# Long-convolution block with adaptive norm: the first norm, the filter's first block and the first convolution interleaved on two-sided pools

## The chip, the core and the metric

The kernel runs on one core of one Trainium2 chip. A core has TensorE (PE, matrix products, with its weight load shown apart as PEld), VectorE (DVE), ScalarE (ACT), GpSimd (POOL) and SyncE (SP, which here only starts transfers). Each engine takes its own instructions in order and waits on semaphores for the others. The metric is device time in microseconds of one execution; the median of three runs counts. Times of places in the trace are microseconds from the first instruction.

## What is computed

One input of 2048 positions by 576 channels runs through a convolution block and a feed-forward block. Each has a norm in front, scaled and shifted by vectors made from a condition, and a gated sum behind. Cut to what matters:

```python
mod = (_silu(c) @ w_mod).reshape(c.shape[0], 6, 1, -1)
sa, ca, ga, sb, cb, gb = (mod[:, i] for i in range(6))
h = _layernorm(x) * (1 + ca) + sa
# per channel: dt = exp(log_dt), A = -exp(log_A_real) + i A_imag, C = (C_real + i C_imag) dt
K = 2.0 * einsum("dn,dnl->dl", C, exp(A * dt * pos)).real      # 128 states, 2048 positions
y = irfft(rfft(h, 4096) * rfft(K, 4096))[:2048] + h * D_skip
x = x + ga * y
h = _layernorm(x) * (1 + cb) + sb
x = x + gb * (relu(h @ w1) @ w2)                               # 576 to 4608 to 576
```

## The kernel before

The 2048 positions are cut into four blocks of 512, each held as 128 partitions by four. The convolution is done by blocks: block s takes the spectra of filter blocks 0 to s and of input blocks s to 0. The 576 channels are in two halves of 288, called p.

**Filter, first block** (`KGen.first`). The filter's 512 first values per channel come from two tables of powers of exp(A dt): W2 (32 powers) and W1 (16 powers, scaled by C). The channels are cut into six groups g of 96, taken two by two (`CHUNKS`). For a pair, `raw` makes on ACT the phases' integer parts and on DVE their fractions (`turns`, L116), then the exponentials on ACT (`exps`). `values` of a group takes sines and cosines on ACT, multiplies them by the exponentials on DVE (L151, L152, the sines' half, read from PSUM) and on POOL (the cosines' half, recorded at L59) and stores W2 and a small table zs through SP's queue. In its odd half, `start` (L167) makes W1's first entry; POOL computes a product called tc for it at L178 and DVE adds at L158. `make` doubles W1 four times (`doubling`, L224 to L228, the last step's sums on POOL), stores W1, and lets PE form 384 products of 32 by 16 (`products`, L236). `rows` copies them out of PSUM, and after three groups `store` writes half a filter block to memory (kd). Everything that goes through `KGen.act` and `KGen.pool` keeps its order on its engine; the rest of every engine's stream is ordered by the framework's planner from the program's order and its own estimate of readiness.

**Modulation** (`Body.mod`). Three weight slices are loaded at the start; sigmoid, the broadcast `cb` and the products for ga, ca and sa (L517) stand in the program after the first `raw`. ca and sa already hold the factor ga. The other three vectors are made later (`mod_late`, L519), each with a load on POOL's queue into a single buffer wm.

**First convolution** (`conv(0)`, from `main`). It begins when `first` has ended and the pools of KGen are closed; new pools lie where those lay, and each new tile waits for the old tiles under it. Its order: x2 is loaded on SP; `norm1` takes statistics, square roots (ACT, kept in order) and two DVE passes for h (L728, L729); `transform` of K for half 0, then of U (that is h) for both halves, each of eight products with copies on ACT (L642, L643); `butterfly` in two halves on DVE (L656 to L670); `product` of the spectra (L812 to L818, six ops of 1152 columns); `inverse` (L839 on PE, a DVE addition into x2 at L844); the same for half 1, whose K uses `transform1` (a transform with half of the butterfly done by PE, L681 and L683). Then comes the second norm (L876 to L920), with transposes on PE, which gives the feed-forward part its input xh, xl and xs. The filter's half 1 is loaded by `load_kt` once kd has been written. Spectra are saved on POOL's queue for later blocks: Ud, Rd and, for K, a second copy in Kd.

**Feed-forward part** (`ffn`). For each of 4 times 36 slices of the hidden width, 14 products for the hidden values (L982) and 14 for the output (L1007). Between them `step` lets a share of the other work through: the filter's other blocks (`KGen.rest`) and the convolutions of blocks 1 to 3.

The lines that tie the first convolution to the filter are these:

```python
            with ExitStack() as c2:
                kg.open(c2)
                setup = kg.setup(I)
                last = kg.first(setup, self.mod(kg))
            self.main(ctx, kg, last)
```

Of the kernel before, what the change touches and what calls it, by code (L numbers as in the profile page):

```python
# [18 lines left out]
P = 128  # L19
# [27 lines left out]
class KGen:  # L47
# [13 lines left out]
    def open(self, ctx):  # L61

        pool = lambda n, **kw: ctx.enter_context(self.tc.tile_pool(name=n, bufs=1, **kw))
        self.pa, self.pc, self.pt, self.pw = (pool(f"kg_{x}") for x in "actw")
        self.ps, self.ph = pool("kg_ps", space=PSUM), pool("kg_ph", space=PSUM)
        self.Zp = self.ps.tile([P, 2, 8 * G], F32, name="Zp")
# [31 lines left out]
    def exps(self, w, m):  # L98

        n = len(EXPS[m])  # L100
        e = self.pt.tile([P, 8, 2 * G], F32, tag="E", bufs=6, name=f"E_{w.start}")[:, :n]
        for i, slot in enumerate(EXPS[m]):
            self.act(e[:, i], self.a[:, w], AF.Exp, scale=float(slot))
        return e

    def turns(self, w):

        F = []
        for slots in TURNS:
            n = len(slots)  # L110
            k = self.pa.tile([P, 8, 2 * G], I32, tag="k", bufs=3, name=f"k_{w.start}")
            k = k[:, :n]
# [9 lines left out]
    def abs(self, f):  # L122
        c = self.pt.tile([P, 8, G], F32, tag="c", bufs=3, name="c")[:, : f.shape[1]]
        self.act(c, f, AF.Abs)
        return c
# [4 lines left out]
    def half_values(self, g, W2, E, f, odd):  # L130
# [8 lines left out]
        for u in range(2):  # L139
            s = self.ps.tile([P, 512], F32, tag="s", bufs=2, name=f"s_{2 * g + u}")  # L140
# [26 lines left out]
    def start(self, g, s15, c15):  # L167

        v, p = self.nc.vector.tensor_tensor, self.pool
# [4 lines left out]
        t = self.pc.tile([P, 2, 2, H], F32, tag="Tc", name="tc")  # L174
# [3 lines left out]
        p(t, cc, c15.unsqueeze(1).broadcast_to(cb), op=ALU.mult)  # L178
        for u in range(2):
# [3 lines left out]
        return (  # L183
            (W1[:, :, 0, 0], t[:, 0], T[:, 1], ALU.add),
# [59 lines left out]
    def first(self, setup, mod):  # L244

        nc, k = self.nc, self.k
        self.W1, self.Z, W2s, EF, ke = {}, {}, {}, {}, {}

        def raw(c):
            w = slice(CHUNKS[c][0] * G, CHUNKS[c][1] * G)  # L250
            F, E = self.turns(w), [None] * 5
            for m in (2, 3, 0, 1, 4):
                E[m] = self.exps(w, m)
                if m in (3, 1):
                    yield
            for g in range(*CHUNKS[c]):
                gs = slice((g - CHUNKS[c][0]) * G, (g - CHUNKS[c][0]) * G + G)
                EF[g] = [e[:, :, gs] for e in E], [f[:, :, gs] for f in F]

        def values(g, then):  # L260
# [8 lines left out]
            for u in range(2):  # L269
                nc.sync.dma_start(  # L270
                    out=strips(k.W2d[2 * g + u], 4),
                    in_=W2[u].rearrange("p r (y b) c -> p (r y) (b c)", y=2),
# [6 lines left out]
        def make(g):  # L279
            self.doubling(g)  # L280
            for u in range(2):
                nc.sync.dma_start(
                    out=strips(k.W1d[2 * g + u], 2),
                    in_=self.W1[g][:, u].rearrange("p (y a) r c -> p y (a r c)", y=2),
                )
            ps = self.bank(f"kps_{g}")[:, :384].rearrange("p (q a) -> p q a", a=16)
            for u in range(2):
                self.products(ps, self.W1[g], W2s[g][u], u)

            def rows():  # L290
                if g % 3 == 0:
                    ke[0] = self.pc.tile([P, 16, 72], F32, tag="ke", bufs=1, name=f"ke_{g}")
                qs = slice(24 * (g % 3), 24 * (g % 3) + 24)
                self.act(ke[0][:, :, qs], ps.rearrange("p q a -> p a q"), AF.Copy)
                if g % 3 == 2:
                    self.store(0, g // 3, ke[0].rearrange("p a q -> p (a q)"), nc.sync)

            return rows

        next(mod)  # L300
        for _ in raw(0):
            pass
        next(mod)
        setup()
        rows = [lambda: next(mod), lambda: next(mod)]
        for c, (a, b) in enumerate(CHUNKS):
            for g in range(a, b):
                values(g, rows.pop(0) if g > a else lambda: None)
            rows.pop(0)()
# [880 lines left out]
```

## Time and profile before

| what | value |
|---|---|
| runs | 1440.12, 1443.22 and 1445.3 us; median 1443.22 us |
| profiled execution | 1442.42 us; its span 1440.7 us, mean granted PE clock 0.925 |
| busy over the span | PE 1239.4, PEld 982.6, DVE 880.7, ACT 498.3, POOL 189.3 us |
| 0 to 28 us | DVE busy 11.4, ACT 19.6, POOL 2.7 us |
| 28 to 45 us | DVE busy 12.7, ACT 15.7, POOL 14.6 us |
| 110 to 145 us | PE busy 13.2, DVE 29.3, ACT 13.0, POOL 26.8 us |
| 1416 to 1441 us | PE busy 15.7, DVE 4.4 us |
| transfers | 346.49 MB, mean 241 GB/s |

How to read it: a row of the profile has the line of the kernel, the engine, the operation, "out<-in" by the program's tile names, the tiles' sizes and the count, then the busy time and the mean length of one, and after the bar the engine's idle time ahead of these instructions with what ended most of it. A row in order of time begins with its start and its length in microseconds; in brackets stands the idle time ahead of it. A row by stretches begins with the stretch, then its length, each engine's busy time with the number of instructions, the granted PE clock, the mean share of the DMA engines and GB/s. A row of transfers ends with the microseconds from issue to landing.

### The profile page before, as it was taken

Reading aid. Unit: us, or ns where it says so; the run is one execution under the profiler, and the core shown is the slowest. Engines: PE = TensorE matmul, PEld = TensorE weight load, DVE = VectorE, ACT = ScalarE, POOL = GpSimd, SP = SyncE. Lnnn points to the kernel's source line nnn. Section 1 sums busy time; section 2 is a strip of 40 time slices with the busy share of each in tenths; the row PEclk is TensorE's granted clock in tenths of the full one; section 3 lists DMA queues with packets and bytes.
Section 4 is the critical chain, followed back from the end, with each engine's and each line's share of the span. In section 5 each row is a group of like instructions: output and inputs, shape, how many; then the busy total and the mean of one; then the engine's idle time right before and its main releaser. Section 6 shows DMA issues by size and latency. Waiting matters only on the chain. (4 is left out here: it accounts for less than half of the span.)

```text
span 1440.7 us, 25957 instructions
## 1 busy us (share of the span) xinstructions
PE 1239.4 (86%) x10600; PEld 982.6 (68%) x10600; DVE 880.7 (61%) x1355; ACT 498.3 (35%) x1002; POOL 189.3 (13%) x273
## 2 busy tenths in 40 slices
PE   2423376999989997788999999989999999999997
PEld 1323354777867775566787778767887878888885
DVE  4988488899756688837936779353889431101101
ACT  7784041322221340252234322634322253223221
POOL 2467211010111111011110110010100000000000
PEclk9655587899999999899999999999999999999998
DMA  4666869387698695659877998575989656666661
GB/s 152 230 232 232 271 223 329 99 288 244 209 368 314 212 325 175 241 166 394 287 256 258 336 322 290 162 237 151 370 307 334 203 154 205 205 199 195 197 190 59
DMA packets 135110, 346.49 MB, mean 241 GB/s; under 512 B 23440, under 2 KB 23728, under 8 KB 134992
## 3 DMA queue, kind: packets, MB, share of 16 engines
q1 hardware_dynamic: 107008, 218.82, 46.7%
q0 software_dynamic: 27696, 125.43, 24.0%
q8 instruction: 83, 1.36, 0.4%
q10 hardware_dynamic: 288, 0.59, 0.1%
q14 instruction: 35, 0.29, 0.1%
HBM read 261.04 MB, written 83.76 MB: 239 GB/s over the span
## 5 line engine op out<-in xcount | busy, mean ns | idle before, releaser
L1007 PE MATMUL acc<-hh,w 128*128 128x512 f32 x1296 | 422.4, 400 | 3.0 <-DVE w L968 2.9
L982 PE MATMUL hps<-xh,w 128*128 128x512 f32 x1152 | 398.5, 406 | 0.0
L988 DVE SCALAR_TENSOR_TENSOR hl<-hps,hh 128x512 fp32r<-128x512 f32 x144 | 99.0, 687 | 319.5 <-ACT hh L987 319.2
L1007 PEld LDWEIGHTS acc<-hh,w 128*128 128x128 f32 x1296 | 243.8, 190 | 56.3 <-DVE w L968 3.3
L1007 PE MATMUL acc<-hl,w 128*128 128x512 f32 x720 | 281.3, 401 | 0.1
L982 PEld LDWEIGHTS hps<-xh,w 128*128 128x128 f32 x1152 | 219.7, 192 | 47.3 <-ACT xh L914 0.3
L982 PE MATMUL hps<-xl,w 128*128 128x512 f32 x576 | 232.9, 404 | 0.0
L987 ACT ACTIVATE hh<-hps 128x512 fp32r<-128x512 f32 x144 | 86.0, 598 | 330.4 <-PE hps L982 327.8
L965 ACT ACTIVATE w<-r 128x576 fp32r<-128x576 f32 x144 | 98.9, 687 | 276.9 <-PE acc L1007 216.5
L1007 PEld LDWEIGHTS acc<-hl,w 128*128 128x128 f32 x720 | 136.3, 190 | 29.6 <-DVE hl L988 0.5
L982 PEld LDWEIGHTS hps<-xl,w 128*128 128x128 f32 x576 | 110.2, 191 | 24.1 <-DVE xl L919 0.4
L982 PE MATMUL hps<-xs,w 128*128 128x512 f32 x288 | 104.4, 427 | 19.8 <-ACT w L956 6.6
L956 ACT ACTIVATE w<-r 128x640 fp32r<-128x640 f32 x144 | 105.5, 733 | 36.1 <-DMA L1d<-w 29.4
L236 PE MATMUL kps<-W,W 128*32 128x16 f32 x2304 | 39.8, 219 | 89.6 <-POOL W L59 55.1
L236 PEld LDWEIGHTS kps<-W,W 128*32 128x32 f32 x2304 | 37.6, 151 | 92.1 <-POOL W L59 56.0
L380 PEld LDWEIGHTS kps<-W1r,W2r 128*32 128x32 f32 x3456 | 67.6, 146 | 35.8 <-issue 21.8
L380 PE MATMUL kps<-W1r,W2r 128*32 128x48 f32 (+2 forms) x3456 | 76.5, 238 | 13.0 <-issue 7.4
L818 DVE TENSOR_TENSOR Y<-Y,T 128x1152 f32<-128x1152 f32 x64 | 84.6, 1349 | 0.1
L982 PEld LDWEIGHTS hps<-xs,w 128*128 128x128 f32 x288 | 54.7, 193 | 36.7 <-DVE w L958 7.5
L643 ACT ACTIVATE Z<-ps_f 128x288 f32<-128x288 f32 x120 | 48.3, 413 | 69.0 <-PE ps_f L642 68.3
L1108 POOL DMA_DIRECT2D out_dram<-x x16 | 8.8, 548 | 475.6 <-DVE x L1106 475.6
L642 PE MATMUL ps_f<-kt,fcK 128*128 128x288 f32 x112 | 39.8, 449 | 13.6 <-DVE kt L756 9.6
(200 smaller groups left out, 1422.5 us busy)
## 6 DMA issues: line engine op xcount, KB each, us to landing
r<-in_w_dram SPq DMA_DIRECT2D x144, 320.0 KB, 4.0
r<-in_w_dram SPq DMA_DIRECT2D x144, 288.0 KB, 3.8
w<-L1d SPq DMA_DIRECT2D x108, 320.0 KB, 3.1
w<-L2d SPq DMA_DIRECT2D x108, 288.0 KB, 3.4
W2r<-W2d POOLq DMA_DIRECT2D x18, 1536.0 KB, 10.0
W2d<-W SPq DMA_DIRECT2D x12, 1536.0 KB, 7.5
Ua<-Ud POOLq DMA_DIRECT2D x15, 1152.0 KB, 11.6
W<-W1d POOLq DMA_DIRECT2D x18, 768.0 KB, 9.2
```

The lines of the kernel that those rows point to most:

```text
L236: self.nc.tensor.matmul(ps[32 * dd : 32 * dd + 32, 12 * u + q, :], W2[:, r, :, ch], W1[:, u, :, r, ch], start=(r == 0), stop=(r == 1),)
L380: nc.tensor.matmul(ps[32 * dd : 32 * dd + 32, q, :], W2[:, r, :, ch], W1[:, :, r, ch], start=(r == 0), stop=(r == 1),)
L642: nc.tensor.matmul(o, fc[:, n2, c, :], src(n2), start=True, stop=True)
L643: ev = nc.scalar.activation(Z[:, n2, c], ps[:, :PC], AF.Copy)
L818: v(y, y, T, op=op or ALU.add)
L956: nc.scalar.activation(w[:, 0], r, AF.Copy)
L965: nc.scalar.activation(w[:, 0:D], r, AF.Copy)
L982: nc.tensor.matmul(ps, a, x, start=(i == 0), stop=(i == 13))
L987: nc.scalar.activation(hh, ps, AF.Relu)
L988: nc.vector.scalar_tensor_tensor(hl, ps, 0.0, hh, op0=ALU.max, op1=ALU.subtract)
L1007: nc.tensor.matmul(acc[i], a, x, start=(f == 0 and j in (0, 3, 6, 9, 12)), stop=(f == NF - 1 and j in (2, 5, 8, 11, 13)),)
L1108: nc.gpsimd.dma_start(out=ov[:, n2], in_=x2[:, n2])
```

## The change

- **Pools.** KGen's pools are split. What only the values need (phases, exponentials, the cosines' buffers, the sines' PSUM banks) lies on the left side and is closed early (`early`); W2, W1, the doublings' tiles and the products' PSUM lie on the right side and are closed `late`, inside the first convolution. The feed-forward part's pools then take the right side.
- **First norm.** x is loaded on SP right behind mod's weights. mod runs in front of the first values. The statistics stand ahead of the first values; square roots and the centering (now four ACT ops) stand in the second `raw`; the factor ca and the summand sa become eight POOL ops of 576 columns: two tiles in the second `raw`, one after each of the next two doublings.
- **tc** moves from POOL to DVE.
- **Order.** The transforms of U and K of half 0 stand ahead of the doublings and products of group 4, group 5's doubling stands behind them; then the butterflies of U and K; then group 5's products.
- **Stores.** W2 of group 5 and W1 of groups 4 and 5 are held back until x2 has been asked for, which happens after U's transform of half 1 (x2 and h share a tile).
- **First convolution.** Written out as `conv0` with four fixed spectrum tiles and two PSUM pools (two banks, then four). Kd of block 0 is Rd of block 0, so its second copy is gone. The later blocks' code loses its cases for s = 0.

The core of the diff:

```diff
-    def open(self, ctx):
+    def open(self, early, late):
...
+        self.pa, self.ss = pool(early, "kg_a", "left"), pool(early, "kg_s", "left", space=PSUM)
+        self.pw, self.pc, self.pt = (pool(late, f"kg_{x}", "right") for x in "wct")
+        self.ps, self.ph = (pool(late, f"kg_{x}", "right", space=PSUM) for x in ("ps", "ph"))
...
-        p(t, cc, c15.unsqueeze(1).broadcast_to(cb), op=ALU.mult)
...
+            (t, cc, c15.unsqueeze(1).broadcast_to(cb), ALU.mult),
...
         def raw(c):
             w = slice(CHUNKS[c][0] * G, CHUNKS[c][1] * G)
+            if c == 1:
+                scale()
+            F = self.turns(w)
+            if c == 1:
+                for i in range(4):
+                    center(i)
+                for i in range(2):
+                    affine(i)
+            E = dict((m, self.exps(w, m)) for m in (2, 3, 0, 1, 4))
...
+        def save(dst, src, held):
+            if held:
+                k.held.append((dst, src))
+            else:
+                nc.sync.dma_start(out=dst, in_=src)
...
+        load, stats, scale, center, affine = norm
         next(mod)
+        load()
+        raw(0)
+        for _ in mod:
             pass
         setup()
+        stats()
+        values(0, lambda: None)
+        values(1, lambda: None)
+        for g in (0, 2):
+            raw(g // 2 + 1)
+            for i in (g, g + 1):
+                double(i)
+                if g == 0:
+                    affine(i + 2)
+                multiply(i)
+            values(g + 2, lambda: None)
+            values(g + 3, lambda: rows(g))
+            rows(g + 1)
+        yield
+        double(4)
+        multiply(4)
+        double(5)
+        yield
+        multiply(5)
+        rows(4)
+        rows(5)
...
+        def center(i):
+            kg.act(h[:, i], h[:, i], AF.Identity, scale=rs[i][:, 3:4], bias=rs[i][:, 4:5])
+
+        def affine(i):
+            kg.pool(h[:, i], h[:, i], self.m["ca"], op=ALU.mult)
+            kg.pool(h[:, i], h[:, i], self.m["sa"], op=ALU.add)
...
+    def conv0(self, ctx, c, first, late):
...
+        kt = [self.load_kt(0, 0)]
+        for t, a in zip((fcKn, gcn), I["neg"]):
+            nc.sync.dma_start(out=t, in_=a)
...
+        run(self.transform(lambda n2: hv[:, n2, :, 0], self.fcU, ZU))
+        run(self.transform(src_K(0), self.fcK, ZK))
+        next(first)
+        W = S(2, "W")
+        run(self.butterfly1(ZU, W))
+        U0 = S(0, "U0")
+        run(self.butterfly2(W, U0, -1))
+        self.save(self.Ud[0][0], U0)
...
+        K0 = S(1, "K0")
+        run(self.butterfly2(W, K0, -1))
+        self.save(self.Rd[0][0], K0)
+        next(first, None)
+        kt.append(self.load_kt(0, 1))
+        Z1 = S(2, "Z1")
+        run(self.transform(lambda n2: hv[:, n2, :, 1], self.fcU, Z1))
+        x2 = self.x2[0] = self.x2p[0].tile([P, 4, D], F32, tag="x2", bufs=1, name="x2_0")
+        kept(nc.sync.dma_start(out=x2, in_=I["x"][0].rearrange("n m d -> m n d")))
+        for dst, src in self.held:
+            kept(nc.sync.dma_start(out=dst, in_=src))
+        late.close()
+        self.ff = self.pool(ctx, "ff", side="right")
+        self.xp = [self.pool(ctx, "xa", side="right")]
+        self.cv = cvb = self.pool(c, "cvb")
+        self.cps, self.nps = self.pool(c, "cpsb", space=PSUM, side="right"), 4
...
+        run(self.product(Y, K0, U0, True))
+        V = S(3, "V0")
+        run(self.butterfly1(Y, V))
+        W, U1 = X("W"), None
+        run(self.butterfly1(Z1, W))
+        U1 = S(2, "U1")
+        run(self.butterfly2(W, U1, -1))
+        self.save(self.Ud[0][1], U1)
+        mod = self.mod_late()
+        next(mod)
...
+        run(self.inverse(x2, 0, ops))
+        W = S(1, "WK")
+        run(self.transform1(src_K(1), self.fcK, fcKn, W))
+        K1 = S(0, "K1")
+        run(self.butterfly2(W, K1, -1))
+        self.save(self.Rd[0][1], K1)
+        next(mod)
+        Y = X("Y1")
+        run(self.product(Y, K1, U1, True))
+        W = S(3, "W")
+        run(self.butterfly1(Y, W))
+        next(mod)
+        V1 = S(1, "V1")
+        run(self.butterfly2(W, V1, 1))
+        run(self.inverse(x2, 1, lambda n2: [(g(n2, c), V1[:, n2, c]) for c in range(2)]))
+        next(mod, None)
+        run(self.norm2(0, x2, self.xp[0]))
```

More of the change, by code (lines that the diff above doesn't have):

```diff
@@ L287, in make, with multiply @@
+        def multiply(g):
+            kps[g] = self.bank(f"kps_{g}")[:, :384].rearrange("p (q a) -> p q a", a=16)
             for u in range(2):
[L288 to L296, printed above, removed]
@@ L794, in pair @@
                 return Ka, Ua
-            order = [0, s, *range(1, s)] if s else [0]
+            order = [0, s, *range(1, s)]
             nxt = pair(0)
@@ L853, in conv @@
         ZK, ZU = self.spec("Z"), None
[L854 to L858 removed]
+        yield from both(self.norm1(x2, h), mm_K(0, ZK))
         kt[1] = self.load_kt(s, 1)
```

325 lines of the change are left out of this document (164 added, 161 removed).

## The prediction, made before the changed kernel was run

> **What bounds the kernel now.** I read the page first, for the shares and the forty slices, then the table by stretches, then DVE's and PE's rows in order of time.
>
> ```profile
> span 1440.7 us, 25957 instructions
> PE   2423376999989997788999999989999999999997
> DVE  4988488899756688837936779353889431101101
> ```
>
> PE is nearly full from the eighth slice on and half empty before it. So the span is a prelude plus a stretch that PE fills.
>
> ```profile
> core 0: us, PE busy (x) PEld busy (x) DVE busy (x) ACT busy (x) POOL busy (x), PEclk, DMA share, GB/s
> 64.00:110.00 46.00, 13.19 (x768) 12.44 (x768) 39.06 (x90) 32.38 (x90) 27.52 (x38) 0.50 0.59 216
> 145.00:177.00 32.00, 13.40 (x768) 12.68 (x768) 10.85 (x24) 0.49 (x1) 8.73 (x11) 0.50 0.82 279
> 177.00:257.00 80.00, 54.33 (x305) 38.65 (x306) 66.61 (x133) 25.14 (x69) 12.20 (x18) 0.78 0.78 269
> 257.00:1416.00 1159.00, 1110.56 (x7864) 882.83 (x7864) 687.55 (x923) 369.10 (x656) 89.28 (x127) 0.98 0.73 245
> ```
>
> From 257 to 1416 PE is busy for 1110.6 of 1159 us. The change edits nothing there, so I carry that stretch over whole: whatever the first matmul of the feed-forward part gains, the end gains. In 64 to 110 DVE works 39 of 46 us; in 145 to 177 no engine is busy for half of the time. That is the hole, and these rows show its edges:
>
> ```profile
> 154.50 0.95 DVE L225 TENSOR_TENSOR T<-W,Zp 128x768 f32<-128x768 f32 x1
> 176.43 0.32 DVE L523 COPY cb<-ct 128x160 f32<-128x160 f32 x1 [20.98 <-PE kps L236]
> 237.47 0.45 DVE L670 TENSOR_TENSOR V<-W 128x288 f32<-128x288 f32 x1
> 256.66 1.22 PE L982 MATMUL hps<-xs,w 128*128 128x512 f32 x2 [0.27 <-DVE xs L917]
> 174.52 1.87 PE L236 MATMUL kps<-W,W 128*32 128x16 f32 x102 [4.16 <-issue]
> ```
>
> DVE stands still for 21 us, until the last products end at 176.4 (174.52 plus 1.87). I call that moment T. From T to the first feed-forward matmul at 256.7 pass 80.3 us. The change can win from the hole and from the 80.3, and pays where it moves T.
>
> **The change, part by part.** *a) First norm first.* Its statistics (eight of 0.44 us) and mod's products go ahead of the first values. There DVE has a gap of 8.7 us:
>
> ```profile
> L483 DVE TENSOR_SCALAR ex<-ex 128x5 f32<-128x5 f32 x1 | 0.2, 171 | 8.7 <-ACT ex L56 8.7
> 75.22 0.50 ACT L56 ACTIVATE s<-k 128x384 f32<-128x384 f32 x1 [10.82 <-DVE W L152]
> 179.82 1.28 ACT L700 ACT_TABLE_LOAD   x1 [20.96 <-DVE mv L699]
> ```
>
> I cost it at nothing. Without that cover (x landing too late) it would be about 4 us of DVE. ACT gets one more table load (1.28), four square roots, and four centerings of 576 columns: some 5 us, ahead of a wait of 10.8 us for DVE, so nothing either; were the wait gone, 5. The table loaded at 179.82 also served the second norm; in the change the sines come between, so that norm pays 1.28 us anew, on the path.
>
> *b) The affine half of the norm moves to POOL, one product (tc) from POOL to DVE.*
>
> ```profile
> L59 POOL TENSOR_TENSOR W<-c,E 128x384 f32<-128x384 f32 x36 | 35.9, 1033 | 0.0
> L59 POOL TENSOR_TENSOR tc<-cc,c 128x192 f32<-128x192 f32 x6 | 3.7, 611 | 6.9 <-ACT c L56 6.9
> L158 DVE TENSOR_TENSOR W<-tc,Tc 128x96 f32<-128x96 f32 x12 | 2.5, 250 | 11.8 <-POOL tc L59 11.8
> L116 DVE SCALAR_TENSOR_TENSOR k<-th,k x66: 340/345/4186, 11.7 to 101.4; 128x192 f32<-128x192 f32 x66
> 45.00:49.00 4.00, 3.92 (x1) 1.00 0.90 307
> 49.00:55.30 6.30, 5.99 (x22) 0.53 1.02 384
> ```
>
> From 192 to 384 columns POOL's op grows by 0.42 us, so 576 columns are about 1.45, and eight of them 11.6 us. The last two rows are of L116 alone: between 45 and 49, with POOL working through the first values, a single one gets through, and its longest lasts 4.19 us; when POOL is quiet, 22 pass in 6 us. Both its inputs lie in SBUF. The first four affine ops (5.8 us) fall into the second chunk's 22 of these. Cost: 0 if POOL comes after them, 5.8 if DVE stands for all of it; I take 4, since some turns pass before POOL starts.
> The Trainium skill, "SBUF — State Buffer", section "Who interferes with whom", has it that a VectorE instruction with two SBUF inputs and a GpSimd one that reads SBUF exclude each other for a whole instruction. By that rule one L116 slips through per POOL op and the four affine ops would cost about 4.4 us, where the row of 45 to 49, with one for four POOL ops, says 5.8.
> Without tc, DVE loses waits of 11.8 us in all, but runs six products with two SBUF inputs of its own, each between 0.35 (L116's undisturbed size) and 4.2 us (its longest). Besides, the last affine stands ahead of the third group's POOL work and delays it by 2.9, less 0.6 for tc, and ACT waits for that work's buffers. Bounds: 8 us of gain, 14 of loss. I take 0, as values is paced by POOL either way.
> So the last doublings start at 140.7 in place of 136.7: +4 us.
>
> *c) Forward transforms ahead of the last products.* The stores of the last factors (two of W2, four of W1) are held back, and PE's products look like this:
>
> ```profile
> 110.00:132.60 22.60, 13.19 (x768) 12.45 (x768) 0.65 0.48 182
> 145.00:176.50 31.50, 13.40 (x768) 12.68 (x768) 0.50 0.83 283
> fcU<-in_fcu_dram SPq DMA_DIRECT2D x1, 512.0 KB, 7.1
> fcK<-in_fck_dram SPq DMA_DIRECT2D x1, 512.0 KB, 9.2
> DMA to landing us min/median/max: 4.2/8.6/13.1
> 185.96 5.82 PE L642 MATMUL ps_f<-kt,fcK 128*128 128x288 f32 x16 [9.57 <-DVE kt L756]
> 191.62 7.92 PE L642 MATMUL ps_f<-h,fcU 128*128 128x288 f32 x32
> ```
>
> 768 products take 22.6 us with the DMA engines at 0.48 and 31.5 at 0.83, for the same 13 us of work; the rest are pauses without a releaser in the trace. With six stores gone but matrices, kt and two saves there, I take 25 (bounds 22.6 and 31.5). Three transforms run from 185.96 to 199.54, 4.5 us each; two are 9. On SP the loads stand behind the last zs store, so they go out near 147: fcU lands at 154, fcK at 157, kt (fifth row, both its loads) between 152 and 161. Products of group 4 are ready at 149.5 (145.5 + 4). PE's queue runs in order, so it may wait there: 0 to 11 us, I take 2. T = 149.5 + 25 + 9 + 2 = 185.5, which is 9.1 later than now.
>
> *d) What is left behind T.* Queued behind the load of kt on SP stands x2, which needs the tile that h held, free only when the third transform is done (T + 4.5).
>
> ```profile
> 182.36 1.12 SPq L321 DMA_DIRECT2D kd<-ke  x2
> 185.45 0.37 SPq L925 DMA_DIRECT2D kt<-kd  x1
> x<-in_x_dram SPq DMA_DIRECT2D x1, 1152.0 KB, 11.6
> L656 DVE TENSOR_TENSOR W<-Z 128x576 f32<-128x576 f32 x6 | 4.5, 749 | 4.2 <-ACT Z L643 4.2
> L667 DVE TENSOR_TENSOR U<-W 128x288 f32<-128x288 f32 x2 | 0.9, 443 | 0.0
> L818 DVE TENSOR_TENSOR Y<-Y,T 128x1152 f32<-128x1152 f32 x4 | 5.3, 1344 | 0.0
> ```
>
> kd goes out at T + 1, kt 3.1 later, landing from T + 8 to T + 17. x2 goes at T + 5 and lands at T + 12 to T + 17; the four PSUM banks of the first inverse's sums wait for it, and K1's transform for a bank: T + 15. It has 32 matmuls, at 0.28 each 9 us: T + 24. A half butterfly is four ops of 0.67 (0.75 less overlap) or two such and four of 0.37: 2.7 and 2.8. Product: six of 1.27, 7.6. So K1 ends at T + 26.5 (its half, partly under the transform), the product at T + 34, its butterflies at T + 39.5; U0, K0, the first product and V0 (21 us of DVE) fill the hole before and around T. From V's end at 237.9 (237.47 + 0.45) to 256.7 pass 18.8; less 1.1 for the gb product that stood ahead of the inverse until 239.0 (its row is with rival C), plus 1.3 for the table: 19. First feed-forward matmul at T + 58.5 (bounds 52 and 66), in place of T + 80.3.
>
> *Sum.* b and c move T by +9.1, d gives 80.3 - 58.5 = 21.8: together 12.7 us of gain. One copy of K less is saved per half; those stores lay on POOL's queue beside DVE's work and count as nothing. The profiled execution took 1442.4 us (span 1440.7 and 1.7 around it), 0.8 below the median of 1443.2. 1442.4 - 12.7 = **1430 us**.
>
> **The rivals.** *A, everything hides.* POOL's affine falls between the turns, loads land early, T stays at 177 and the chain is 52.5: 229.5, a gain of 27, **1415 us**. For it: the hole is real; against it: L116's row.
>
> *B, the feeds are late.* PE's queue holds the products behind K0's transform, kt takes 13.1 again (147 + 13 = 160), products keep their 31.5 us: T = 160 + 4.5 + 31.5 less 2 already done = 194, the first feed-forward matmul at 252.5, a gain of 4.2: **1438 us**. For it: both durations stand in the rows; against: six stores fewer.
>
> *C, slower: mod's late weights behind the held stores.* The place: PE's queue, ahead of the second inverse.
>
> ```profile
> W2d<-W SPq DMA_DIRECT2D x12, 1536.0 KB, 7.5
> W1d<-W SPq DMA_DIRECT2D x12, 768.0 KB, 5.4
> wm_cb<-in_w_mod_dram POOLq DMA_DIRECT2D x1, 1152.0 KB, 6.9
> wm_gb<-in_w_mod_dram POOLq DMA_DIRECT2D x1, 1152.0 KB, 10.8
> 235.17 3.86 PE L534 MATMUL mps_gb<-wm_gb,cb 128*32 128x128 f32 x50 [4.33 <-DMA wm_gb<-in_w_mod_dram]
> ```
>
> The held stores are two of the first row and four of the second, 6.1 MB, at the 280 GB/s of the products' last stretch 22 us from T + 13: if wm lies where the last W1 lay, its first load waits until T + 35. Two loads of 6.9 to 10.8 us and two products of 3.9 follow in turn, as there is one wm buffer: cb's product ends between T + 56.5 and T + 64, while V is ready at T + 39.5. The inverse waits behind it, and the first feed-forward matmul comes 19 later, at T + 75.5 to T + 83, or 261 to 268.5: 1447 to 1454, say **1450 us**. It decides once cb's product ends later than T + 52. For it: mps_gb waited 4.3 us for such a load; against: the tile may lie elsewhere.
> The Trainium skill, "DMA: Bandwidth & Descriptors", section "Issuing engines are not separate DMA queues", says that transfers started by SP and by POOL interleave on the same engines; by that the held stores slow wm's loads even where its tile is free. kt's 4.2 and 13.1 agree.
>
> *D, the change doesn't do what it says.* The planner orders each engine's stream, so products may still go first. Then T = 174.5, three transforms follow, and DVE's sequence (two butterflies, product, V0, U1, K1's half, product, butterflies) ends near 222: 241, a gain of 16, **1426 us**.
>
> **How the numbers follow.** Main 0.43, A 0.13, D 0.12, B 0.17, C 0.15. The likeliest says 1430, by itself 1422 to 1437. To leave out no more than 2 in 10 the range goes from 1411 (A with 4 us to spare) to 1445 (B with T 7 us later still), which leaves out C. A change under 0.3%, 4.3 us here, can't be told from none. Faster: A, D, nearly all of the main case and over half of B, 0.77. Same: 0.11, the rest of B and of the main case and the low end of C, 0.03. Slower: 0.12, the rest of C.
>
> **What would show it.** Right: the first feed-forward matmul near 244; no wait of DVE for kps over 5 us; T near 185; x2's landing between T and K1's transform. b is wrong if the second chunk's L116 end by 56, c if the 768 last products take over 30 us or PE waits over 5 us for kt, d if the chain behind T is over 66 us, above all if PE waits for a wm tile. All of it is wrong if the feed-forward stretch isn't 1159 us long within 3.

## The result and the profile after

| | median | runs | ratio to the kernel before, 95% interval |
|---|---|---|---|
| before | 1444.04 us | 20 | |
| after | 1448.4 us | 20 | 1.0030, 1.0015 to 1.0044 |
| after, measured again later | 1449.3 us (before: 1442.1) | 12 | 1.0054, 1.0033 to 1.0074 |

The change makes the kernel slower by 4 to 7 us. The forecast was 1430, with a range that ended at 1445. The page and the table by stretches of the changed kernel, for the same stretches as before:

```profile
span 1445.4 us, 25948 instructions
...
DVE  5988657899756679837936789363899332110101
...
145.00:177.00 32.00, 24.02 (x794) 18.28 (x794) 22.66 (x42) 7.08 (x17) 8.94 (x9) 0.87 0.43 145
177.00:257.00 80.00, 49.97 (x277) 34.25 (x278) 45.71 (x83) 17.86 (x47) 9.54 (x14) 0.70 0.78 268
```

The hole before T was filled: in 145 to 177 DVE is busy for 22.7 us (10.9 before) and PE for 24.0 (13.4 before). But DVE's work in 177 to 257 fell from 66.6 to 45.7 us without the stretch getting shorter: what was pulled forward left idle time behind. PE's, DVE's and ACT's rows in order of time, with the wait ahead of each in brackets, show where:

```profile
178.15 0.41 PE L243 MATMUL kps<-W,W 128*32 128x16 f32 x6 [2.67 <-issue]
196.00 5.92 PE L894 MATMUL ps_i<-V,gc 128*128 128x288 f32 x12 [10.12 <-DVE V L698]
213.38 1.33 PE L723 MATMUL ps_f<-kt,fcK 128*128 128x288 f32 x2 [6.62 <-DVE x L899]
237.75 3.86 PE L572 MATMUL mps_cb<-wm_cb,cb 128*32 128x128 f32 x50 [8.36 <-DMA wm_cb<-in_w_mod_dram]
258.08 0.73 PE L1108 MATMUL hps<-xs,w 128*128 128x512 f32 x2 [0.73 <-DVE xs L946]
...
170.44 0.46 DVE L712 TENSOR_TENSOR K<-W 128x288 f32<-128x288 f32 x1
186.99 0.45 DVE L974 TENSOR_TENSOR kt<-kt,dsk 1x288 f32<-1x288 f32 x1 [16.10 <-DMA kt<-kd]
187.37 2.61 DVE L878 TENSOR_TENSOR Y<-K,U 128x1152 f32<-128x1152 f32 x2
209.46 0.82 DVE L1084 TENSOR_TENSOR w<-r,w 128x640 fp32r<-128x640 f32 x1 [11.52 <-ACT w L1082]
...
208.69 1.51 ACT L1082 ACTIVATE w<-r 128x640 fp32r<-128x640 f32 x2 [22.37 <-DMA r<-in_w_dram]
```

T is 178.15 + 0.41 = 178.6, only 2.2 later than before. U and K of half 0 are ready at 170.9, yet DVE stands 16.1 us in front of a 0.45 us addition into the second kt (`src_K(1)`), which cannot land before the products have ended; the first product (L878) is queued behind it. Then DVE stands 11.5 us in front of the first split of a feed-forward weight (L1084: ACT rounds the raw weight r to w, DVE takes the rest); r is late. The additions of the first inverse are queued behind that (x2 had landed at 192.5), K1's transform needs the PSUM banks that they empty, and so it starts at 213.4. V1 is ready at 241.3, where it was 237.9. From T to the first feed-forward matmul pass 79.5 us: 80.3 before, 58.5 in the forecast.

SP's own queue says why r is late:

```profile
185.90 0.39 SPq L996 DMA_DIRECT2D x<-in_x_dram  x1
186.38 1.01 SPq L998 DMA_DIRECT2D W2d<-W  x2
187.49 7.88 SPq L998 DMA_DIRECT2D W1d<-W  x4
195.42 2.88 SPq L1066 DMA_DIRECT2D r<-in_w_dram  x2
```

The six held stores go out right behind x2 and take the queue until 195.4; only then r is asked for, and it lands at 208.7 among 6.1 MB of stores. In 145 to 177 the DMA engines are at 0.43, where they were at 0.82 before.

So the prelude gains nothing (first feed-forward matmul at 258.1, before at 256.7). That leaves 1184.0 us from there to the end before (1440.7 - 256.7) and 1187.3 after (1445.4 - 258.1), in a part that the change all but leaves alone (7932 matmuls in both). The last feed-forward block, in which PE never waits, shows it. First the rows of the same 100 us, before and after; then where the 14 first matmuls of one slice begin and where the next kind begins, before and after:

```profile
1300.00:1400.00 100.00, 100.00 (x443) 82.84 (x442) 11.06 (x16) 30.07 (x48) 0.00 (x0) 1.00 0.66 197
...
1286.56 0.61 PE L982 MATMUL hps<-xs,w 128*128 128x512 f32 x2
...
1289.73 0.62 PE L1007 MATMUL acc<-hh,w 128*128 128x512 f32 x2
```

```profile
1300.00:1400.00 100.00, 100.00 (x434) 81.32 (x433) 10.55 (x16) 29.46 (x47) 0.00 (x0) 1.00 0.66 194
...
1282.45 0.63 PE L1108 MATMUL hps<-xs,w 128*128 128x512 f32 x2
...
1285.72 0.63 PE L1133 MATMUL acc<-hh,w 128*128 128x512 f32 x2
```

At the same granted clock of 1.00 PE gets through 434 matmuls in place of 443. The 14 first matmuls take 3.27 us in place of 3.17, 233.6 ns each in place of 226.4. From the third block's evacuation (its sums leaving PSUM) to the last one's pass 228.7 us after and 224.9 before.

### The profile page after: what moved, and what is told of

Same layout as the page of the kernel before. It is cut to its first block, busy times and chain, and to the rows that moved or that the text cites. A ratio compares the mean times of both kernels' runs of the same rounds, so it can differ in the third digit from the quotient of the medians.

```text
span 1445.4 us, 25948 instructions
## 1 busy us (share of the span) xinstructions
PE 1250.2 (86%) x10600; PEld 981.7 (68%) x10600; DVE 878.0 (61%) x1353; ACT 503.5 (35%) x1007; POOL 197.8 (14%) x271
## 5 line engine op out<-in xcount | busy, mean ns | idle before, releaser
L1108 PEld LDWEIGHTS hps<-xs,w 128*128 128x128 f32 x288 | 54.6, 192 | 34.8 <-issue 7.8
L687 ACT ACTIVATE Z<-ps_f 128x288 f32<-128x288 f32 x104 | 42.4, 408 | 65.3 <-PE ps_f L686 65.2
L686 PE MATMUL ps_f<-h,fcU 128*128 128x288 f32 x128 | 47.2, 471 | 14.1 <-DVE W L235 14.0
```

Of the source, the lines that this page charges most:

```text
L686: nc.tensor.matmul(o, fc[:, n2, c, :], src(n2), start=True, stop=True)
L687: nc.scalar.activation(Z[:, n2, c], ps[:, :PC], AF.Copy)
L1108: nc.tensor.matmul(ps, a, x, start=(i == 0), stop=(i == 13))
```

## The experiments

Theories on the prelude: **1**, the addition ahead of the first product alone ate the gain; **2**, the held stores did, by way of r and of mod's weights. On the feed-forward part: **P**, the start addresses of its tiles, which the pools' new side moved; its rival, the order of the work. All results in one table. "T to first" is from the end of the last product to the first feed-forward matmul in the run's profile, "last block" from the third evacuation to the fourth. Each run has one profile; a0 is the changed kernel once more, and its "T to first" is 3.2 us shorter, so gains of that size in this column say nothing.

| run | median us | ratio, 95% interval | first feed-forward matmul | T to first | last block |
|---|---|---|---|---|---|
| before | 1444.0 | 1 | 256.7 | 80.3 | 224.9 |
| after | 1448.4 | 1.0030 (1.0015 to 1.0044) | 258.1 | 79.5 | 228.7 |
| a0_after_again | 1449.3 | 1.0054 (1.0033 to 1.0074) | 255.2 | 76.3 | 228.7 |
| e1_add_late | 1450.2 | 1.0057 (1.0033 to 1.0081) | 259.4 | 77.3 | 228.7 |
| e4_split_late | 1455.5 | 1.0076 (1.0049 to 1.0103) | 256.4 | 75.7 | 228.7 |
| h1_hold_w1 | 1444.8 | 1.0002 (0.9981 to 1.0022) | 253.4 | 71.1 | 228.7 |
| h2_hold_w2 | 1443.1 | 1.0004 (0.9986 to 1.0021) | 246.9 | 68.4 | 228.8 |
| e2_no_hold | 1437.6 | 0.9965 (0.9946 to 0.9985) | 246.9 | 67.7 | 228.7 |
| p1_pad | 1446.3 | 1.0023 (1.0007 to 1.0039) | 257.8 | 79.3 | 224.9 |
| p2_no_hold_pad | 1434.5 | 0.9952 (0.9933 to 0.9971) | 243.4 | 64.3 | 224.9 |
| x4_x2_split | 1432.0 | 0.9931 (0.9904 to 0.9958) | 248.7 | 66.6 | 225.0 |
| bx_mixed (on before) | 1448.3 | 1.0050 (1.0030 to 1.0071) | 257.1 | 80.9 | 228.8 |
| bp_off32 (on before) | 1440.8 | 0.9990 (0.9978 to 1.0002) | 258.5 | 81.8 | 225.0 |
| b0_no_affine | 1447.3 | 1.0045 (1.0027 to 1.0062) | 257.1 | 79.0 | 228.7 |

**e1_add_late.** The addition stands behind the first product and V.

```diff
-            v(ktv[0:1, 0, :, 0], ktv[0:1, 0, :, 0], dv, op=ALU.add)
+            d = v(ktv[0:1, 0, :, 0], ktv[0:1, 0, :, 0], dv, op=ALU.add)
+            if p:
+                kept(d)
...
         run(self.butterfly1(Y, V))
+        src1 = src_K(1)
...
-        run(self.transform1(src_K(1), self.fcK, fcKn, W))
+        run(self.transform1(src1, self.fcK, fcKn, W))
```

> One edit to the changed kernel: the add that completes the second kt on VectorE is put behind the first product and the first V, where it stood ahead of them with 16.1 us of waiting. Theory 1 (this head-of-line wait alone ate the gain): the first inverse starts near 187 in place of 202, the chain behind it moves with it, and the first feed-forward matmul comes at 240 to 245 in place of 258; time 13 to 18 us below the changed kernel's. Theory 2 (the held stores decide: they keep the loads of r and of mod's weights back): the first inverse does start near 187, but VectorE then stands in the split of the feed-forward weight (waiting for r, which lands near 208) and mod's cb product still ends near 241, so the first feed-forward matmul comes at 254 to 258; time 0 to 4 us below. Rival (neither; TensorE's own stream sets the end): the first inverse does not move by more than 3 us.

Its rows of DVE in order of time:

```profile
173.92 2.62 DVE L878 TENSOR_TENSOR Y<-K,U 128x1152 f32<-128x1152 f32 x2
190.48 0.45 DVE L974 TENSOR_TENSOR kt<-kt,dsk 1x288 f32<-1x288 f32 x1 [5.97 <-DMA kt<-kd]
212.50 0.82 DVE L1087 TENSOR_TENSOR w<-r,w 128x640 fp32r<-128x640 f32 x1 [12.76 <-ACT w L1085]
```

The first product runs 13.5 us earlier and the first inverse starts at 188.5 in place of 196.0 (the 202 of the expectation is where its first twelve matmuls end), but DVE meets the split all the same and waits there until 212.5; the fourth addition of the first inverse stands behind it. Theory 1 falls: nothing reaches the end.

**e4_split_late.** As e1, and the first split is kept behind the second norm.

```diff
-                nc.vector.tensor_tensor(w[:, 1], r, w[:, 0], op=ALU.subtract)
+                d = nc.vector.tensor_tensor(w[:, 1], r, w[:, 0], op=ALU.subtract)
+                if g < 1:
+                    self.tc.keep_in_program_order(d)
```

> Two edits to the changed kernel: the add that completes the second kt is put behind the first product and V, and the first split of the feed-forward weight behind the second norm; the stores stay held. Theory 1 with the second block counted in (two head-of-line waits on VectorE ate the gain): K1's transform starts near 197 in place of 213, and the first feed-forward matmul comes at 238 to 245; time 13 to 20 us below the changed kernel's. Theory 2: VectorE is free of both waits and V1 ends near 226, 15 us earlier than now, but the second inverse stands behind cb's product on TensorE, which waits for mod's weights behind the held stores until 237 to 241; the first feed-forward matmul stays at 254 to 258 and the time within 4 us of the changed kernel's, with a wait of TensorE for wm_cb over 10 us.

```profile
212.89 0.22 DVE L1099 TENSOR_TENSOR w<-r,w 128x64 fp32r<-128x64 f32 x1 [14.27 <-DMA r<-in_w_dram]
```

The next split, of the output weights, now stands in front of the fourth addition and waits as long. Both expectations missed here: V1 did not end near 226 but at 239.8, as this wait took the place of the one removed. Besides, the first feed-forward matmuls then waited 4 us for the split that was put off, and the run is the slowest; whether by this alone isn't shown.

**e2_no_hold.** Nothing is held.

```diff
-                    W2[u].rearrange("p r (y b) c -> p (r y) (b c)", y=2), g == NG - 1,
+                    W2[u].rearrange("p r (y b) c -> p (r y) (b c)", y=2), False,
...
-                    self.W1[g][:, u].rearrange("p (y a) r c -> p y (a r c)", y=2), g > NG - 3,
+                    self.W1[g][:, u].rearrange("p (y a) r c -> p y (a r c)", y=2), False,
```

> One edit to the changed kernel: the six last stores (two of W2, four of W1) are not held back but go out at once, as in the kernel before. Theory 1: if VectorE's add still stands ahead of the first product, its wait stays over 10 us and nothing is gained; the products run with the DMA engines busier, so T is 182 to 190 in place of 178.6 and the time is 0 to 8 us above the changed kernel's. Theory 2: T is 2 to 8 us later for the same reason, but r and mod's weights land before they are needed (no wait of VectorE or ScalarE for r over 3 us, no wait of TensorE or GpSimd for a wm tile over 3 us), cb's product ends before 232, and the first feed-forward matmul comes at 240 to 247 in place of 258; time 11 to 18 us below.

PE's and DVE's rows in order of time:

```profile
178.78 0.42 PE L243 MATMUL kps<-W,W 128*32 128x16 f32 x7 [1.66 <-issue]
200.13 1.33 PE L723 MATMUL ps_f<-kt,fcK 128*128 128x288 f32 x2 [5.06 <-DVE x L899]
246.92 0.73 PE L1108 MATMUL hps<-xs,w 128*128 128x512 f32 x2 [0.72 <-DVE xs L946]
...
178.03 2.62 DVE L878 TENSOR_TENSOR Y<-K,U 128x1152 f32<-128x1152 f32 x2
195.35 0.45 DVE L974 TENSOR_TENSOR kt<-kt,dsk 1x288 f32<-1x288 f32 x1 [6.73 <-DMA kt<-kd]
203.54 0.81 DVE L1084 TENSOR_TENSOR w<-r,w 128x640 fp32r<-128x640 f32 x1
```

This one edit brings 11 us at the first feed-forward matmul and as much at the end: faster than the kernel before. The split finds r there. T is 179.2: holding the stores had bought 0.6 us (the products took 20.7 us in place of 23.6, with the DMA engines at 0.43 in place of 0.75 in 145 to 177, but PE's stretch began 2.0 us later). One caution: the edit also changed the planner's order. The addition for kt now stands behind V, and half of the products ahead of U's transform. So this run takes both waits of DVE off the path, not one. The wait for wm_cb stayed at 10.9 us, against what Theory 2 had said.

**h2_hold_w2 and h1_hold_w1** release one half of the stores each (one of the two lines of e2's edit).

> One edit to the changed kernel: of the six held stores only the two of W2 stay held; the four of W1 go out at once. Theory 2 with the W1 stores as the cause (mod's weights need the place of the last W1, and r's loads stand behind six stores): the wait of GpSimd for W1d ahead of wm_sb shrinks from 36.7 us to under 15, cb's product ends before 234, r lands before 203, and the first feed-forward matmul comes at 246 to 252; time 6 to 11 us below the changed kernel's. Theory 2 with the two W2 stores as enough: r still lands after 203, VectorE waits over 6 us at the split, and the first feed-forward matmul comes at 253 to 258; time 0 to 5 us below. Rival (the holding as such is harmless): within 2 us of the changed kernel's.

> One edit to the changed kernel, the complement of h2_hold_w2: the two stores of W2 go out at once and the four of W1 stay held. The planner then puts three of the first four loads of r ahead of kt on SP, and with them ahead of the held stores; GpSimd's load of wm_sb still waits for the last W1, and VectorE's add for the second kt still stands ahead of the first product. Theory r (what cost was r behind the held stores, by way of the splits that stand ahead of the first inverse's adds on VectorE): no wait of VectorE or ScalarE for r over 4 us after 195, K1's transform starts at 202 to 206 in place of 213.4, the first feed-forward matmul comes at 246 to 250, the time 6 to 11 us below the changed kernel's, although wm_sb waits for W1d as long as before. Theory wm (the rival C of the forecast: mod's weights behind the held W1 stores set the second inverse): cb's product still ends at 239 or later and the first feed-forward matmul comes at 254 to 258. Theory add (the wait for kt): K1's transform starts after 209 and little is gained.

h2 has the first feed-forward matmul at 246.9, like e2, so releasing the four W1 stores is enough. But not because r comes earlier, as its expectation had it (before 203). Its rows of DVE and ACT:

```profile
180.26 0.75 DVE L699 TENSOR_TENSOR V<-Y 128x576 f32<-128x576 f32 x1
193.59 0.45 DVE L974 TENSOR_TENSOR kt<-kt,dsk 1x288 f32<-1x288 f32 x1 [12.59 <-DMA kt<-kd]
201.82 1.18 DVE L899 TENSOR_TENSOR x<-ps_i,x 128x288 f32<-128x288 f32 x3
208.09 0.83 DVE L1084 TENSOR_TENSOR w<-r,w 128x640 fp32r<-128x640 f32 x1 [5.09 <-ACT w L1082]
...
207.32 0.74 ACT L1082 ACTIVATE w<-r 128x640 fp32r<-128x640 f32 x1 [2.26 <-DMA r<-in_w_dram]
```

r lands at 207.3, almost as late as in the changed kernel (208.7), and DVE still waits 12.6 us for kt and 5.1 us for the split. What changed is where they stand: the planner put the addition behind V and the split behind all four additions of the first inverse, so K1's transform starts at 199.2. The same late transfers cost little when nothing that is ready stands behind them. Of its 11 us only about 5 reach the end (1.0004 against 1.0030 and 1.0054); its feed-forward part was 1194.8 us long in the one profile, and why isn't shown.

In h1 the planner puts three of r's loads and their splits early (SP asks for them at 158.5, 185.1 and 186.3), while W1 still goes out late, at 191.4. Its rows of DVE, POOL and PE:

```profile
188.00 0.82 DVE L1084 TENSOR_TENSOR w<-r,w 128x640 fp32r<-128x640 f32 x1 [6.86 <-ACT w L1082]
193.94 0.45 DVE L974 TENSOR_TENSOR kt<-kt,dsk 1x288 f32<-1x288 f32 x1 [1.32 <-DMA kt<-kd]
194.31 2.61 DVE L878 TENSOR_TENSOR Y<-K,U 128x1152 f32<-128x1152 f32 x2
235.70 0.45 DVE L712 TENSOR_TENSOR V<-W 128x288 f32<-128x288 f32 x1
...
205.81 0.75 POOL L546 DMA_DIRECT2D wm_sb<-in_w_mod_dram  x1 [23.61 <-DMA W1d<-W]
223.10 0.75 POOL L677 DMA_DIRECT2D Rd<-K  x1 [8.50 <-DVE K L711]
223.85 0.76 POOL L546 DMA_DIRECT2D wm_cb<-in_w_mod_dram  x1
...
233.03 3.86 PE L572 MATMUL mps_cb<-wm_cb,cb 128*32 128x128 f32 x50 [8.83 <-DMA wm_cb<-in_w_mod_dram]
```

Now splits and the addition stand together in front of the first product, which starts at 194.3 although its spectra were ready at 181. K1's transform starts at 212.9, which "theory add" had foretold; yet 8.4 us are gained from T on, about half of them as the transform then runs through in 8.2 us, where in the changed kernel it took 12.9. Theory r missed its own numbers (202 to 206 for that transform, 246 to 250 for the first feed-forward matmul, 6 to 11 us of time), as the planner moved the splits ahead of the first product. The wm theory falls: wm_sb waited 23.6 us for W1, yet cb's product ended at 236.9, 0.7 after V1 (235.7 + 0.45). wm_cb's load stands behind the save of K1 in POOL's queue, and its one buffer is free only when sb's product, which PE does behind K1's transform, has ended; so it starts when K1 is done, whatever W1 does. The cb product ends 0.3 to 0.7 us after V1 in the changed kernel, e1, e2 and h1, and 1.9 us after it in h2.

**p1_pad, bp_off32, bx_mixed: the start addresses.** On the left side, before, all tiles of the feed-forward part started at multiples of 64 bytes. On the right side the built program has the weights w1 at byte 192,992, the inputs of the first and third block at 164,832 (both 32 beside a multiple of 64), and those of the second and fourth at 55,744 (a multiple).

```diff
+        self.pool(ctx, "pad", side="right").tile([P, 8], F32, name="pad")
         self.ff = self.pool(ctx, "ff", side="right")
```

> One edit to the changed kernel: an unused tile of 32 bytes a partition at the top of the right side, so that all tiles of the feed-forward pools there start at a multiple of 64 bytes, as in the kernel before (now they start 32 bytes beside one). Theory P (the start address costs TensorE time): in the last feed-forward block, where nothing else runs on TensorE, the first matmuls (hps) step by 226 to 228 ns in place of 233.6 and the second (acc) by 226 to 227 in place of 228.2; first feed-forward matmul to end 1183 to 1185 us in place of 1187.3; time 2 to 4 us below the changed kernel's. Rival (the order of the work in the blocks makes the difference): both steps stay at 233.6 and 228.2 within 1 ns and the time stays within 1.5 us.

On the kernel before, the same tile stands ahead of `ff` (bp_off32: weights and inputs move together) or ahead of `xb` (bx_mixed: the inputs of the second and fourth block move alone).

> The reverse on the kernel before: the same unused tile of 32 bytes ahead of its feed-forward pool, so that weights and inputs of both matmuls start 32 bytes beside a multiple of 64; no instruction is changed. Theory P: the steps of hps and acc in the last block rise from 226.6 and 226.8 to 228 to 234 ns; first feed-forward matmul to end 1186 to 1189 us in place of 1184.0; time 2 to 5 us above the kernel before. Rival (order, not address): steps unchanged within 1 ns, time within 1.5 us.

> The kernel before with the unused tile of 32 bytes ahead of the pool that holds the inputs of the second and fourth feed-forward block (xb) alone, so that there the weights start at a multiple of 64 bytes and the inputs 32 beside one; no instruction is changed. Theory P2 (what costs is that weights and inputs of one matmul lie 32 bytes apart in their 64; both shifted together cost nothing, as bp_off32 showed): in the last block hps steps by 233 to 234 ns in place of 226.6, the last block takes 228 to 229 us from evacuation to evacuation in place of 224.9, and the time is 3 to 7 us above the kernel before. Rival (only weights off a multiple of 64 with inputs on one cost, or the place on the right side): hps stays at 226 to 228 ns, the last block at 225 us, the time within 2 us of the kernel before.

The row of the same 100 us for p1_pad, bp_off32 and bx_mixed, one fence each:

```profile
1300.00:1400.00 100.00, 100.00 (x443) 82.77 (x442) 11.06 (x16) 30.61 (x48) 0.00 (x0) 1.00 0.67 196
```

```profile
1300.00:1400.00 100.00, 100.00 (x443) 82.81 (x442) 11.06 (x16) 29.93 (x47) 0.00 (x0) 1.00 0.67 196
```

```profile
1300.00:1400.00 100.00, 100.00 (x435) 81.23 (x434) 10.76 (x16) 29.70 (x47) 0.00 (x0) 1.00 0.65 193
```

p1 gets the 443 matmuls back and its last block takes 224.9 us. bp_off32 misses Theory P as first put: everything 32 bytes off costs nothing. bx_mixed then settles it: not one instruction differs from the kernel before, only the place of some inputs, and PE gets through 435, the last block takes 228.8, the time rises by 0.5%. What counts is that weights and inputs of one matmul lie 32 bytes apart within 64. The end of p1 doesn't show it: its feed-forward part took 1187.7 us in the one profile, where 1183 to 1185 had been expected, and its median is still above the kernel before (1.0023), its interval overlapping that of the changed kernel. The profile has 3.7 us more than before in the second block (319.1 in place of 315.4 us), a part that varies by 7 us between the profiles here. Over all profiles the feed-forward part is 1182 to 1188 us long in the five with equal places (mean 1184.7) and 1187 to 1197 in the nine with unequal ones (mean 1191.8); a difference of 7.1 us, where two blocks with unequal places would give 7.6 by the last block's 3.8.

**p2_no_hold_pad and x4_x2_split.** Both remedies together; x4 also cuts the load of x2 in four.

```diff
-        kept(nc.sync.dma_start(out=x2, in_=I["x"][0].rearrange("n m d -> m n d")))
+        for n2 in range(4):
+            kept(nc.sync.dma_start(out=x2[:, n2], in_=I["x"][0][n2]))
```

> The two edits together: nothing held, and the unused tile of 32 bytes. If the two causes are independent: first feed-forward matmul at 245 to 249 as with nothing held, first feed-forward matmul to end 3 us shorter than there (1186 to 1188 in place of 1190.5), time 1432 to 1436, 8 to 12 us below the kernel before. If the address is not what the steps come from: 1436 to 1439.

> p2_no_hold_pad (nothing held, unused tile of 32 bytes) with the load of x2 cut into four of a quarter each, in the same place of the queue. If x2's landing as a whole at 198 is what K1's transform waits for: the first quarter lands at 193 to 196, the transform starts at 195.5 to 196.5 in place of 198.6, and the first feed-forward matmul comes at 240 to 242 in place of 243.4. Rival (kt, which lands at 194.6, and mod's cb product at 228.8 hold the chain anyway): the first feed-forward matmul stays at 242.5 to 244.5 and the time at 1432 to 1436.

Both beat both kernels: 0.5% and 0.7% below before, 0.8 to 1.2% below the changed kernel. In p2 and in x4 K1's transform starts 19.5 us after T (198.6 - 179.1; 201.6 - 182.1), so cutting x2's load did nothing on this path: kt's landing holds it, as the rows of p2 show. Between the two DVE does U1's first butterflies and one addition.

```profile
194.67 0.45 DVE L974 TENSOR_TENSOR kt<-kt,dsk 1x288 f32<-1x288 f32 x1 [6.02 <-DMA kt<-kd]
198.61 1.33 PE L723 MATMUL ps_f<-kt,fcK 128*128 128x288 f32 x2 [3.51 <-DVE x L899]
```

x4's first feed-forward matmul, 248.7, lies outside both of its expectations, as T itself came 3.0 us later there. The difference of their medians lies within their intervals.

**b0_no_affine.**

```diff
-            kg.pool(h[:, i], h[:, i], self.m["ca"], op=ALU.mult)
-            kg.pool(h[:, i], h[:, i], self.m["sa"], op=ALU.add)
+            pass
```

> The changed kernel with GpSimd's eight instructions of the first norm's affine half left out, so the first convolution's input is only centred and scaled; the rest is as it was. Step b of the forecast (they stand in VectorE's way for about 4 us): the second chunk's turns end at 50 to 52 in place of 55.1 and the last doublings start near 132 in place of 135.8. Rival (they are covered by GpSimd's own gaps): last doublings at 135 to 136.5, the time within 2 us of the changed kernel's.

The start of the last doublings without the affine half, in DVE's rows in order of time:

```profile
135.54 0.35 DVE L231 TENSOR_TENSOR t<-W,Zp 128x192 f32<-128x192 f32 x1
```

In the changed kernel this row stands at 135.77: 0.2 us for all eight instructions. They are covered. POOL's rows of the changed kernel show where the first of them fell:

```profile
53.15 3.32 POOL L59 TENSOR_TENSOR h<-h,m_ca 128x576 f32<-128x576 f32 x1 [3.87 <-ACT h L56]
56.55 1.41 POOL L59 TENSOR_TENSOR h<-h,m_sa 128x576 f32<-128x576 f32 x1
```

The second chunk's turns had run on DVE since 48.8 and ended at 55.2.

**a0_after_again.**

> The changed kernel itself, unedited, beside the others on one chip: 1446 to 1449, 3 to 6 us above the kernel before; the profile's first feed-forward matmul at 257 to 259.5 and the last block at 228.7 us.

The slow-down came again, 0.54% or 7 us, a little above what was expected. Its first feed-forward matmul came at 255.2, below what was expected: from one profile to the next this place moves by 3 us, which is why the gain of e2 (11) can be read from single profiles and that of x4 over p2 can't.

## Why the prediction was wrong, step by step

- **What bounds it** held: the span is a prelude and a stretch that PE fills. "I carry that stretch over whole" did not: the part from the first feed-forward matmul on took 3.3 us more. It was argued from the instructions, which are the same, and forgot that their tiles move. Moving the pools to the other side put weights and inputs of the second and fourth block 32 bytes apart: 3.8 us in the last block alone, and 3.0 to 7.1 permille of time by bx_mixed on the kernel before. That would be enough for the whole slow-down of 1.5 to 4.4 permille; how much of it is due to the places in the changed kernel itself isn't resolved, as p1, which mends them alone, is still 0.7 to 3.9 permille above the kernel before.
- **a** held as far as the trace goes: the front is as fast as before with the norm in it, and the second norm's table load (at 243.94, 1.28 us) fell into a wait of ACT for the second inverse, so the 1.3 us charged for it in d were not paid.
- **b** was sized at +4 and is 0 (b0; the last doublings at 135.8 in place of 136.7, forecast 140.7). The sign that was named, the second chunk's turns ending by 56, came: they end at 55. The row of 45 to 49 was read rightly, but the affine work met few of the turns: POOL waited for ACT's centering until 53.15, when 2 us of them were left. That is nearly the case that the prediction priced at 0, with POOL behind them. The Trainium skill, "SBUF — State Buffer", section "Who interferes with whom", has VectorE and GpSimd exclude each other on their shared ports; by it the affine instructions would have cost, as an estimate, about 4.4 us if they fell among the turns, and the 0.2 us of b0 says that they don't. Where the two did meet, the trace agrees, and POOL paid: its first affine instruction took 3.32 us, the next 1.41.
- **c**: T was to be 185.5 and is 178.6. The mechanism held (transforms among the first, no wait for kt); the size was off. It began at 146.3 in place of 149.5, as b cost nothing; the products took 20.7 us (152.9 to 155.1 and 160.1 to 178.6) in place of 25; the wait of 2 didn't come; the two transforms took 11.7 in place of 9.
- **d** is the step that failed: "the product, V0 (21 us of DVE) fill the hole before and around T", 58.5 us from T on. It summed DVE's work by what it needs and not by the order in which DVE's stream would have it. Two instructions that wait for late transfers stood in front: the addition into the second kt (16.1 us) and the split of the first feed-forward weight (11.5 us, r behind the held stores). Neither the split nor r was in the sum. So K1's transform began at T + 34.8 in place of T + 15, and that is 19.8 of the 21.0 us by which the way from T on was too short. e1 takes the first away and gains 2 us from T on, less than the 3 that a0 and the changed kernel differ by; h1 takes r's lateness away, leaves the addition in front and gains 8; e2 takes both off the path and gains 12; h2 leaves both transfers late but has both instructions behind the ready work, and gains 11. No run moved the two and nothing else: in e2, h1 and h2 the planner reordered other work too, and in e4 the next split took the place of the first.
- With nothing held and the addresses mended, p2 has its first feed-forward matmul at 243.4, where the forecast had 244, but by two errors that cancel: T 6.3 us earlier than forecast and the chain behind it 5.8 longer. There kt lands at 194.6, T + 15.5, at the late end of the T + 8 to T + 17 given; K1's transform starts at T + 19.5 in place of T + 15 and takes 13.1 us in place of 9; from V1 to the first feed-forward matmul pass 15.0 in place of 19. The Trainium skill, "DMA: Bandwidth & Descriptors", section "Issuing engines are not separate DMA queues", says that transfers interleave on the same engines whichever engine started them. The traces agree: kd, started by SP, takes 2.8 us to land in the changed kernel and 6.3 in h2, where POOL has started the load of wm_sb beside it (7.9 in p2, with r's loads under way too).
- **Rival C** named 1450 us and the held stores, and both came, with the end of cb's product where it had it (T + 63); that was luck, as its mechanism was wrong. It had cb's product wait for W1's place and the inverse for cb, with V ready at T + 39.5; V1 was no earlier than T + 62.8. The wait for W1 exists (36.7 us on POOL) and decides nothing, as h1 shows. What the held stores delay is r, in SP's queue, and that costs what it does because of what stands behind the split in DVE's stream, as h2 shows. Rival D was wrong: U's transform went ahead of all 768 products and K's of 634 of them.

What stays open: why h2's gain is only half there at the end, why p1's end moved so little, and the 5 to 7 us by which each of the first three blocks differs between the profiles.

## What to carry to other kernels

A transfer held back "until there is room" should be followed to the end: list what is queued behind it, who waits for that, and which short instruction of which in-order engine stands in front of long ones because of it. When work is pulled into a hole, sum the receiving engine's stream in its order, with the landing time of every instruction's input, not the work alone; of two waits in one stream, removing the first only shows the second. A late transfer that can't be made earlier can still be made harmless, by putting what waits for it behind the work that is ready. When pools are moved, compare the start addresses of operands that are read together, even where no instruction changes.

## What was not expected of the hardware

A matmul of 128x128 by 128x512 (fp32r) costs 226 to 227 ns in a stream when weights and moving input start alike modulo 64 bytes, whether at 0 or at 32, and 233 to 234 when one is at 0 and the other at 32: 3%, at a granted clock of 1.00, in five kernels with equal and eight with unequal places, in both directions (after: weights at 32; bx_mixed: inputs at 32). The Trainium skill, "SBUF — State Buffer", section "Who interferes with whom", gives TensorE one read port for the moving operand and one for the weights, independent of each other; by that rule the places would not matter to each other, and the rows of 434 and 443 matmuls say that they do. Other places than 0 and 32 were not tried, and why they matter isn't shown.
